# From unit 4 on, two units share one SSD stretch on TensorE; the recurrent half of Y in 32x64 tiles, the first MLP matmul in 512 columns, PSUM banks chosen step by step, and a new order from unit 3

## The chip, the cores and the metric

One core of a Trainium2 chip runs one program. The figure of merit is device time per execution in microseconds (us), a median of several runs. The engines are TensorE (PE in the profile; its weight loads are PEld), VectorE (DVE), ScalarE (ACT), GpSimd (POOL) and SyncE (SP), which issues nearly all DMAs. Each engine works through its own instructions in the order in which they were written, and waits where a semaphore tells it to. TensorE writes only to PSUM, here eight banks of 128 partitions by 512 fp32 columns.

## The reference

Two stages follow each other. The first is a chunked state-space scan (SSD) over x of shape (4 batches, 8 heads, 768 steps, 32 features) with state size 16:

```python
L = np.exp(cum[:, :, :, None] - cum[:, :, None, :]) * causal
M = np.einsum('bhin,bhjn->bhij', Cc, Bc) * L
y_intra = np.einsum('bhij,bhjd->bhid', M, xc)
y_inter = np.einsum('bhin,bhnd->bhid', Cc, state) * np.exp(cum)[..., None]
y = y_intra + y_inter
state = decay_full * state + sum_j B_j x_j decay_from_j
```

Its output, regrouped to 3072 tokens by 256 columns, goes through an MLP: `h = x @ w_in` (256 to 2048), `g = gelu_tanh(h)`, `out = g @ w_out` (2048 to 256), fp32 in HBM, bf16 on TensorE.

## The kernel before, in words

The kernel uses chunks of 128 steps: 24 chunks in 4 batches, two chunks to a unit, so 12 units of T = 256 tokens. Unit u holds chunks 2u and 2u+1; a batch is three units. The decays are folded into B and C beforehand (`mul`), so that the SSD part of a unit is plain matmuls:

- **G.u** (`f_G`): C times B per head pair, weights of 32 rows by 128 columns, 256 columns streamed, eight matmuls into the PSUM pair ga, gb. **M.u.0** and **M.u.1** on VectorE mask ga and gb into bf16.
- **D.u** (`f_D`): the chunk's contribution to the state, four matmuls per chunk (none for a batch's last chunk). **S.u.k** (`f_S`, VectorE) adds it to the running state; **SP.c** (`f_SP`, VectorE) spreads the state of chunk c over the heads in bf16.
- **Y.u** (`f_Y`): per chunk eight matmuls of the masked scores with x (intra) and, unless the chunk is a batch's first, eight of the spread state with C (inter), all with weights of 128 rows by 32 columns and 128 streamed columns, accumulated in the bank yb. **yev.u** evicts the bank to xm, the MLP's input.
- **s1.u.i** (`f_s1`, i = 0 to 7): the first MLP matmul, four matmuls of 256 columns into one bank of pool hp (two buffers). **gelu.u.i** on ScalarE evicts that bank to gT.
- **s2.u.k.q** (`f_s2`): a quarter of the second MLP matmul of chunk 2u+k, four matmuls of 256 columns into a bank o_ps (in the last four chunks partly yb). **oev.c** evicts chunk c's result, **store.c** writes it to HBM.
- For batches 2 and 3, B and C are prepared through DRAM: **load_bc.b** reads them, **mul** scales them, **load_wr** writes the scaled copy to DRAM, **load_tr** reads it back transposed (ch, bh), **load_bn** reads it back untransposed (bn, which D needs), and **F.b** on VectorE splits ch into ce, which G needs.

Every one of these pieces is a named step. The string ORDERED lists all steps in the order in which their instructions are written, with the engine where there is a choice (`:A`, `:D`, `:P`). Nothing else sets the order within an engine. The framework adds the semaphore waits that the tiles' reads and writes call for. From unit 3 on, before, Y.u, D.u+1 and G.u+1 are welded into one step, so that each unit has one SSD stretch on TensorE between steps of the MLP.

In the code before, `f_G` is around L618, `f_D` L651, `f_Y` L673 and L682, `f_S` L697 and L699, `f_SP` L706, `f_s1` L732, `f_gelu` L736, `f_s2` L750, `f_store` L760, and L337, L339 and L341 are the copies on ScalarE, GpSimd and VectorE.

Of the kernel before, what the change touches and what calls it, by code (L numbers as in the profile page):

```python
# [1001 lines left out]
```

## Time and profile before

| | |
|---|---|
| time, median of 3 runs | 117.47 us (116.52 to 118.22) |
| span of the profiled execution, first to last instruction | 115.0 us |
| TensorE busy | 108.1 us, 94% of the span |
| VectorE, ScalarE, GpSimd busy | 68.0, 70.0, 25.9 us |
| granted TensorE clock | 1.000 throughout |

The profile gives one execution. Its span leaves out what lies ahead of the first and behind the last instruction; the three timed runs lie 1.5 to 3.2 us above that span, and the profiled execution has no time of its own beside it. "Busy" of TensorE counts from a matmul's issue to the modelled end of its result, which is later than the moment at which the next matmul may start: the distance between the starts of consecutive matmuls is the pace, and the duration is the pace plus the way through the array.

### The profile page before, as it was taken

Reading aid. Unit: us, or ns where it says so; the run is one execution under the profiler, and the core shown is the slowest. Engines: PE = TensorE matmul, PEld = TensorE weight load, DVE = VectorE, ACT = ScalarE, POOL = GpSimd, SP = SyncE. Lnnn points to the kernel's source line nnn. Section 1 sums busy time; section 2 is a strip of 40 time slices with the busy share of each in tenths; the row PEclk is TensorE's granted clock in tenths of the full one; section 3 lists DMA queues with packets and bytes.
Section 4 is the critical chain, followed back from the end, with each engine's and each line's share of the span. In section 5 each row is a group of like instructions: output and inputs, shape, how many; then the busy total and the mean of one; then the engine's idle time right before and its main releaser. Section 6 shows DMA issues by size and latency. Waiting matters only on the chain.

```text
span 115.0 us, 3377 instructions
## 1 busy us (share of the span) xinstructions
PE 108.1 (94%) x1421; PEld 91.7 (80%) x1421; DVE 68.0 (59%) x136; ACT 70.0 (61%) x133; POOL 25.9 (23%) x54
## 2 busy tenths in 40 slices
PE   6979888999999999999999999999999999999990
PEld 2235566888879997989989899889898898999970
DVE  6889998989974755969448491186750851010100
ACT  3159687687654455747675876456495576758620
POOL 7636856806439020201120030000000000000000
PEclk9999999999999999999999999999999999999999
DMA  0999979979994779997556922350003020001113
GB/s 24 231 309 336 332 212 191 317 132 321 215 238 101 141 177 203 196 272 175 88 131 150 209 62 85 111 86 0 0 9 134 0 71 26 0 0 55 42 62 120
DMA packets 43103, 16.00 MB, mean 139 GB/s; under 512 B 36688, under 2 KB 41552, under 8 KB 43088
## 3 DMA queue, kind: packets, MB, share of 16 engines
q1 hardware_dynamic: 42896, 15.70, 55.3%
q8 instruction: 11, 0.18, 0.7%
q10 hardware_dynamic: 192, 0.09, 0.3%
q14 instruction: 4, 0.03, 0.1%
HBM read 11.07 MB, written 3.93 MB: 130 GB/s over the span
## 4 chain that ended last, share of the span: by engine, by line
PE 82%; DVE 5%; DMA 4%; SPq 3%; issue 2%; ACT 2%; DVEq 0%
PE hp L732 35%; PE o_ps L750 34%; DMA x_t<-in_x_dram 4%; PE yb L750 3%; PE yb L673 3%; PE ga L618 2%; PE yb L682 2%; DVE m L628 1%; DVE sp_new L706 1%; SPq L164 1%; ACT gT L736 1%; SPq L151 1%; SPq L160 1%; DVE rt L364 1%; DVE r_t L354 1%
## 5 line engine op out<-in xcount | busy, mean ns | idle before, releaser
L736 ACT ACTIVATE gT<-hp 128x512 bf16<-128x512 f32 x96 | 54.3, 596 | 28.9 <-PE hp L732 28.6
L732 PE MATMUL hp<-xm,w_in_sb 128*128 128x256 bf16 x384 | 53.4, 273 | 1.1 <-DVE s_new L699 0.5
L750 PE MATMUL o_ps<-w_out_sb,gT 128*128 128x256 bf16 x352 | 46.8, 273 | 0.0
L732 PEld LDWEIGHTS <-w_in_sb 128*128 128x128 bf16 x384 | 41.2, 114 | 4.0 <-issue 2.7
L750 PEld LDWEIGHTS <-gT 128*128 128x128 bf16 x384 | 37.4, 98 | 4.1 <-issue 0.4
L341 DVE COPY o_sb<-o_ps 128x256 f32<-128x256 f32 x12 | 5.1, 425 | 26.9 <-PE o_ps L750 26.9
L628 DVE TENSOR_TENSOR m<-ga,tri 128x1024 bf16<-128x1024 f32 x12 | 14.6, 1216 | 0.0
L628 DVE TENSOR_TENSOR m<-gb,tri 128x1024 bf16<-128x1024 f32 x11 | 13.4, 1216 | 0.0
L339 POOL CAST x<-x_t 128x512 bf16<-128x512 f32 x8 | 6.0, 756 | 28.1 <-DMA x_t<-in_x_dram 24.4
L706 DVE SCALAR_TENSOR_TENSOR sp_new<-s_new,pend,bmask 128x256 bf16<-128x256 f32 x17 | 8.0, 483 | 0.1
L699 DVE SCALAR_TENSOR_TENSOR s_new<-s_new,pend,hp 128x64 f32<-128x64 f32 x13 | 3.5, 272 | 7.4 <-PE hp L651 7.3
L720 PE MATMUL yb<-wz 128*128 128x512 bf16 (+2 forms) x21 | 6.6, 455 | 1.1 <-DVE warm L226 1.1
L337 ACT ACTIVATE o_sb<-o_ps 128x256 f32<-128x256 f32 x10 | 3.8, 383 | 5.1 <-PE o_ps L750 3.8
L682 PE MATMUL yb<-m,x 128*32 128x128 bf16 x192 | 6.1, 220 | 0.0
L337 ACT ACTIVATE xm<-yb 128x512 bf16<-128x512 f32 x8 | 4.8, 596 | 1.3 <-PE hp L651 0.7
L720 PEld LDWEIGHTS <-wz 128*128 128x128 bf16 x21 | 2.3, 116 | 4.1 <-issue 2.1
L673 PE MATMUL yb<-ce,sp_new 128*32 128x128 bf16 x160 | 5.3, 221 | 0.0
L339 POOL CAST w_out_sb<-wf 128x512 bf16<-128x512 f32 x6 | 4.1, 692 | 4.7 <-DMA wf<-in_moe_w_out_dram 4.7
L618 PE MATMUL ga<-ce,bh 32*128 32x256 bf16 x48 | 4.7, 273 | 0.3 <-DVE par L289 0.3
L618 PE MATMUL gb<-ce,bh 32*128 32x256 bf16 x48 | 4.7, 273 | 0.0
L750 PE MATMUL yb<-w_out_sb,gT 128*128 128x256 bf16 x32 | 4.5, 273 | 0.0
L682 PEld LDWEIGHTS <-x 128*32 128x32 bf16 x192 | 3.7, 96 | 0.9 <-issue 0.9
(114 smaller groups left out, 75.0 us busy)
## 6 DMA issues: line engine op xcount, KB each, us to landing
out_dram<-o_sb SPq DMA_DIRECT2D x24, 128.0 KB, 2.0
x_t<-in_x_dram SPq DMA_DIRECT2D x20, 128.0 KB, 3.9
wf<-in_moe_w_in_dram SPq DMA_DIRECT2D x4, 512.0 KB, 7.0
wf<-in_moe_w_out_dram SPq DMA_DIRECT2D x4, 512.0 KB, 7.1
bc_t<-in_C_dram SPq DMA_DIRECT2D x3, 384.0 KB, 4.7
bc_t<-in_B_dram SPq DMA_DIRECT2D x3, 384.0 KB, 5.7
scr<-bc SPq DMA_DIRECT2D x4, 192.0 KB, 2.3
x_t<-in_x_dram SPq DMA_DIRECT2D x1, 512.0 KB, 4.4
```

What stands on the lines that cost most here:

```text
L337: nc.scalar.activation(o, i, AF.Copy)
L339: nc.gpsimd.tensor_copy(out=o, in_=i)
L341: nc.vector.tensor_copy(out=o, in_=i)
L618: nc.tensor.matmul(out=gbank(g)[:, 256 * k:256 * k + 256], lhsT=bh_of(2 * u + k)[gs], rhs=ce_of(2 * u + k)[gs], start=True, stop=True, til ...
L628: nc.vector.tensor_tensor(out=m_of(u)[:, 2 * i:2 * i + 2].rearrange("p g k e t -> p (g k e) t"), in0=gx[i].rearrange("p g (k t) -> p (g k) ...
L673: nc.tensor.matmul(out=y4[32 * j:32 * j + 32, k, w], lhsT=sp[:, 32 * h:32 * h + 32], rhs=ce_of(gc)[:, h % 2], start=first(j), stop=False, ...
L682: nc.tensor.matmul(out=y4[32 * j:32 * j + 32, k, w], lhsT=X16[u][:, k, 32 * h:32 * h + 32], rhs=m[:, h // 2, h % 2, :], start=first(j), st ...
L706: nc.vector.scalar_tensor_tensor(out=sp_new.rearrange("p (g d) -> p g d", g=4), in0=(XN[0][:, H * D:H * D + 64] if gc == 0 else state[("s" ...
L720: nc.tensor.matmul(out=t[:, 0:m * 128], lhsT=wz, rhs=w3.to_broadcast([128, m, 128]), start=True, stop=True, skip_group_check=True)
L732: nc.tensor.matmul(out=hp[:, j * T:(j + 1) * T], lhsT=w_in_k[:, w, q, k], rhs=xm[:, w, u * T:(u + 1) * T], start=(w == 0), stop=(w == 1))
L736: nc.scalar.activation(gts[u][:, 2 * i:2 * i + 2], hps.pop((u, i)).rearrange("p (j t) -> p j t", j=2), AF.Gelu_apprx_tanh)
L750: nc.tensor.matmul(out=ops[gc], lhsT=gts[u][:, fi, k * Q:(k + 1) * Q], rhs=w_out_sb[:, fi, :], start=(fi == 0 and (u > 0 or k == 0)), stop ...
```

## The change

From unit 4 on (`U2 = 4`) units are taken in pairs (4,5), (6,7), (8,9), (10,11):

- Y of a pair becomes **Yi.u** (all intra matmuls, as before 128 rows by 32 columns) for both units and then **YI.u** (all inter matmuls, now weights of 32 rows by 64 columns, four a chunk instead of eight). A pair's Y fills two whole banks, one per half w of the columns, each evicted by one **yew.u.w**, w = 0 on ScalarE and w = 1 on VectorE.
- D of an odd unit from 7 on is written into the bank of the even unit's D, at columns 128 to 255. D of both units stands between Yi and YI of the pair ahead.
- G from unit 6 on is sixteen matmuls of 32 rows by 64 columns instead of eight of 32 by 128. G of the even unit stands behind YI; G of the odd unit stands alone further on, as do G.5 and D.5.
- s1 of a pair is 16 steps of two matmuls of 512 columns, over both units' tokens, instead of 2 times 8 steps of four matmuls of 256. gelu is as large as before.
- The three pools hp (2 banks), o_ps (1) and yb (1) become four fixed banks a, b, o and y; ORDERED names the bank behind an @ where it isn't the usual one.
- ORDERED names the same steps in the same order up to s1.2.6, the step behind oev.0; from there the order is new.

```diff
+    U2 = 4
+    PT = 2 * T
-    GT_BUFS = 5
+    GT_BUFS = 2
-    pso = ctx.enter_context(tc.tile_pool(name="pso", bufs=1, space=bass.MemoryType.PSUM))
-    psh = ctx.enter_context(tc.tile_pool(name="psh", bufs=2, space=bass.MemoryType.PSUM))
...
-    yb = ps1.tile([128, 512], FP32, name="yb")
+    bank = {k: ps1.tile([128, 512], FP32, name=f"bank_{k}") for k in "aboy"}
+    yb = bank["y"]
+    def take(pool):
+        if at:
+            return bank[at.pop(0)]
+        if pool == "hp":
+            hp_turn.append(0)
+            return bank["ba"[len(hp_turn) % 2]]
+        return bank[pool]
...
     def f_G(u):
+        if u > U2 + 1:
+            for k in range(2):
+                for i, g in [(i, g) for i in range(2) for g in range(4)]:
+                    gs, js = slice(32 * g, 32 * g + 32), slice(64 * i, 64 * i + 64)
+                    nc.tensor.matmul(out=gbank(g)[js, 256 * k:256 * k + 256], lhsT=bh_of(2 * u + k)[gs, js],
+                                     rhs=ce_of(2 * u + k)[gs], start=True, stop=True,
+                                     tile_position=(32 * g, 64 * i), skip_group_check=True)
+            return
...
     def f_D(u):
-        DT[u] = psh.tile([128, 512], FP32, name="hp")
+        if u < U2 + 2 or u % 2 == 0:
+            DT["bank"] = take("hp")
+        DT[u] = DT["bank"][:, 0:128] if u < U2 + 2 or u % 2 == 0 else DT["bank"][:, 128:256]
...
+    def f_Yi(u):
+        v = u % 2
+        YT[u] = (take("y"), take("o")) if v == 0 else YT[u - 1]
+        for w, k, j in [(w, k, j) for w in range(2) for k in range(2) for j in range(4)]:
+            h, t = 4 * w + j, v * T + k * Q
+            nc.tensor.matmul(out=YT[u][w][32 * j:32 * j + 32, t:t + Q],
+                             lhsT=X16[u][:, k, 32 * h:32 * h + 32], rhs=MT[u][:, h // 2, k, h % 2],
+                             start=(v == 0 and k == 0), stop=True, tile_position=(0, 32 * j), skip_group_check=True)
+
+    def f_YI(u):
+        for k in range(2):
+            gc = 2 * u + k
+            if gc % CPB == 0:
+                continue
+            sp = state.pop(("sp", gc - 1))
+            t = u % 2 * T + k * Q
+            for g in range(4):
+                gs, i = slice(32 * g, 32 * g + 32), g % 2
+                nc.tensor.matmul(out=YT[u][g // 2][64 * i:64 * i + 64, t:t + Q],
+                                 lhsT=sp[gs, 64 * g:64 * g + 64], rhs=ch_of(gc)[gs], start=False, stop=True,
+                                 tile_position=(32 * g, 64 * i), skip_group_check=True)
+
+    def f_yew(u, w, eng):
+        copy(eng, xm[:, w, u * T:u * T + PT], YT[u][w])
...
+    def f_s1(u, i):
+        gt(u)
+        hp = hps[(u, i)] = take("hp")
+        if u < U2:
...
+        else:
+            q, k = divmod(i, 4)
             for w in range(2):
+                nc.tensor.matmul(out=hp, lhsT=w_in_k[:, w, q, k], rhs=xm[:, w, u * T:u * T + PT],
+                                 start=(w == 0), stop=(w == 1))
...
-    for u in range(3, NU - 1):
-        y = steps[f"Y.{u}"]
-        gone = [steps.pop(f"D.{u + 1}"), steps.pop(f"G.{u + 1}")]
...
-gelu.11.5 store.16 s1.11.7 s2.10.1.3 store.20 oev.21:D gelu.11.6 s2.11.0.1.yb gelu.11.7
+M.5.1 load_bc.3.1 load_bc.3.0 s1.3.6 s1.3.7 s2.2.1.1 store.4 gelu.3.6 gelu.3.7 Yi.4@ya Yi.5 F.2 D.6@b
+SP.10 S.6.0 D.7 mul.3.1:P YI.4 S.6.1 YI.5 G.6 s2.2.1.2 s2.2.1.3 yew.4.1 S.7.0 yew.4.0 s1.4.0@a S.7.1
...
+s2.11.0.2 s2.11.0.3 oev.22:A s2.10.0.3 oev.21:A oev.23:A store.17 oev.20:A store.20 store.23 store.22
+store.21
```

What stands in the engines' queues at three places follows. A row gives the line, the operation, the tile written and read (with the number of its buffer) and what the instruction waits for, an engine or a DMA queue by name; rows that only repeat are left out.

**The SSD stretch on TensorE and the state on VectorE.** First TensorE before, from the end of Y.5 through D.6 (hp_1166) to G.6:

```order
L673 MATMUL yb_148<-ce_712,sp_new_1084 32x128
L682 MATMUL yb_148<-m_1079,x16_967 32x128
L651 LDWEIGHTS bn_1103 [waits Activation_49,DMAHW6_49]
L651 MATMUL hp_1166<-x16_1096,bn_1103 32x64 [waits Pool_49]
L618 LDWEIGHTS bh_1106 [waits DMAHW7_49]
L618 MATMUL ga_146<-ce_1126,bh_1106 128x256 [waits DVE_49]
L618 MATMUL gb_147<-ce_1126,bh_1106 128x256
```

The same place after the change, from the end of Yi.5 through D.6 (x16_930), D.7 (x16_874), YI.4 and YI.5 to G.6:

```order
L717 MATMUL bank_a_142<-m_932,x16_867 32x128
L675 LDWEIGHTS bn_955 [waits Activation_49,DMAHW3_49]
L675 MATMUL bank_b_143<-x16_930,bn_955 32x64 [waits Pool_49]
L675 MATMUL bank_b_143<-x16_874,bn_955 32x64 [waits DVE_49]
L730 MATMUL bank_y_145<-ch_671,sp_new_783 64x128
L730 MATMUL bank_a_142<-ch_671,sp_new_783 64x128
L633 LDWEIGHTS bh_953 [waits DMAHW2_49]
L633 MATMUL ga_140<-ce_1020,bh_953 64x256
```

VectorE after the change at that place: F.2 (twice), SP.10, S.6.0, S.6.1, yew.4.1 and S.7.0.

```order
L548 TENSOR_SCALAR ce_1020<-ch_941,par_116 128x768 [waits DMAHW1_49]
L755 TENSOR_SCALAR sp_new_1031<-s_new_951,pend_128,bmask_110 128x256 [waits DVE_49]
L746 COPY s_new_1033<-bank_b_143 128x64 [waits PE_49,Activation_49]
L748 TENSOR_SCALAR s_new_1053<-s_new_1033,pend_128,bank_b_143 128x64 [waits DVE_49,PE_49]
L351 COPY xm_139<-bank_a_142 128x512 [waits PE_49]
L748 TENSOR_SCALAR s_new_1088<-s_new_1053,pend_128,bank_b_143 128x64 [waits DVE_49]
```

D.7 now follows D.6 in the same bank, with S.6.0 written between the two, and its first matmul carries a wait on VectorE; S.6.1, written behind D.7, waits for TensorE once more. The pairs (6,7) and (8,9) have the same form with D.8, S.8.0, D.9 and D.10, S.10.0, D.11; in the last pair nothing of the kind is left.

**SP's queue ahead of batch 2's transposes.** Before:

```order
L177 DMA x_t_957<-in_x_dram 128x8x32 [waits DMAHW0_49]
L513 DMA scr21_1046<-bc16_949 128x768 [waits DMAHW1_49,Pool_49]
L177 DMA x_t_1061<-in_x_dram 128x8x32 [waits DMAHW2_49]
L177 DMA x_t_1061<-in_x_dram 128x8x32 [waits DMAHW3_49]
L513 DMA scr20_1064<-bc16_949 128x768 [waits DMAHW4_49,Pool_49]
L520 DMA_TRANSPOSE ch_1081<-scr21_1046 128x768 [waits DMAHW5_49,DMAHW1_49]
L525 DMA bn_1103<-scr20_1064 128x6x128 [waits DMAHW6_49,DMAHW4_49]
```

After:

```order
L175 DMA x_t_775<-in_x_dram 128x8x32 [waits DMAHW1_49]
L175 DMA x_t_778<-in_x_dram 128x8x32 [waits DMAHW3_49]
L822 DMA out_0_dram<-o_sb_763 128x256 [waits DMAHW5_49,DVE_49]
L523 DMA scr21_865<-bc16_808 128x768 [waits DMAHW6_49,DVE_49]
L523 DMA scr20_876<-bc16_808 128x768 [waits DMAHW7_49,Pool_49]
L822 DMA out_0_dram<-o_sb_781 128x256 [waits DMAHW0_49,Activation_49]
L530 DMA_TRANSPOSE ch_941<-scr21_865 128x768 [waits DMAHW6_49,DMAHW1_49]
L530 DMA_TRANSPOSE bh_953<-scr20_876 128x768 [waits DMAHW7_49,DMAHW2_49]
L535 DMA bn_955<-scr20_876 128x6x128 [waits DMAHW3_49]
```

The loads of x for units 6 and 7 (two DMAs each) and two stores now stand ahead of the transposes, and bn is read behind both transposes instead of between them.

**The end, on ScalarE and SP.** Before, ScalarE's last two evictions (chunks 22 and 23), and SP's last stores (22, 21, 18, 23):

```order
L337 ACTIVATE o_sb_2239<-yb_148 128x256 [waits DMAHW1_49,PE_49,Activation_49]
L337 ACTIVATE o_sb_2241<-o_ps_2221 128x256 [waits DMAHW2_49,PE_49]
L760 DMA out_0_dram<-o_sb_2239 128x256 [waits DMAHW5_49,Activation_49]
L760 DMA out_0_dram<-o_sb_2205 128x256 [waits DMAHW6_49,DVE_49]
L760 DMA out_0_dram<-o_sb_2037 128x256 [waits DMAHW7_49]
L760 DMA out_0_dram<-o_sb_2241 128x256 [waits DMAHW0_49,Activation_49]
```

After, chunks 22, 21, 23 and 20 on ScalarE, and the stores in the order 20, 23, 22, 21:

```order
L347 ACTIVATE o_sb_1949<-bank_a_142 128x256 [waits DMAHW7_49,DMAHW2_49,PE_49]
L347 ACTIVATE o_sb_1955<-bank_y_145 128x256 [waits DMAHW0_49,Activation_49]
L347 ACTIVATE o_sb_1957<-bank_b_143 128x256 [waits DMAHW5_49,DMAHW1_49,DVE_49]
L347 ACTIVATE o_sb_1960<-bank_o_144 128x256 [waits DMAHW2_49,PE_49]
L822 DMA out_0_dram<-o_sb_1960 128x256 [waits DMAHW5_49,Activation_49]
L822 DMA out_0_dram<-o_sb_1957 128x256 [waits DMAHW6_49]
L822 DMA out_0_dram<-o_sb_1949 128x256 [waits DMAHW7_49]
L822 DMA out_0_dram<-o_sb_1955 128x256 [waits DMAHW0_49]
```

The last four chunks are now evicted by ScalarE one after the other, and the first of the last four stores is that of the chunk that is evicted last. TensorE's last step is s2.10.0.3 (chunk 20), and the step ahead of it s2.11.0.3 (chunk 22).

256 lines of the change are left out of this document (137 added, 119 removed).

## The prediction

> **What bounds the kernel now.** I read the page first.
>
> ```profile
> PE 108.1 (94%) x1421; PEld 91.7 (80%) x1421; DVE 68.0 (59%) x136; ACT 70.0 (61%) x133; POOL 25.9 (23%) x54
> PE 82%; DVE 5%; DMA 4%; SPq 3%; issue 2%; ACT 2%; DVEq 0%
> ```
>
> TensorE is busy 94% of the span and is 82% of the chain that ended last. The waits tell the same: nobody keeps TensorE waiting after the start. So the span behaves as TensorE's queue plus a short tail, and an edit is worth what it takes from that queue or puts into it. TensorE's timeline gives the prices (start, duration; a pace is the distance between starts).
>
> ```profile
> 32.23 0.60 PE L732 MATMUL hp<-xm,w_in_sb 128*128 128x256 bf16 x4
> 43.65 0.60 PE L750 MATMUL o_ps<-w_out_sb,gT 128*128 128x256 bf16 x4
> 44.18 0.29 PE L673 MATMUL yb<-ce,sp_new 128*32 128x128 bf16 x8
> 44.30 0.28 PE L682 MATMUL yb<-m,x 128*32 128x128 bf16 x8
> 44.41 0.28 PE L673 MATMUL yb<-ce,sp_new 128*32 128x128 bf16 x8
> 44.52 0.28 PE L682 MATMUL yb<-m,x 128*32 128x128 bf16 x8
> 44.63 0.20 PE L651 MATMUL hp<-x,bn 128*32 128x64 bf16 x4
> 44.77 0.28 PE L618 MATMUL ga<-ce,bh 32*128 32x256 bf16 x2
> 44.89 0.27 PE L618 MATMUL ga<-ce,bh 32*128 32x256 bf16 x2
> 45.10 0.63 PE L732 MATMUL hp<-xm,w_in_sb 128*128 128x256 bf16 x4
> 110.01 1.91 PE L750 MATMUL o_ps<-w_out_sb,gT 128*128 128x256 bf16 x16
> ```
>
> The last row: sixteen matmuls take 1.91 us with one way through the array (0.27), so 256 columns cost 1.64 / 15 = 0.1092 us, a step of four 0.437. In the SSD stretch eight matmuls of Y cost 0.1125, since four run side by side; D with four costs 0.03, with eight about 0.055; G costs 0.23 (0.12 from one chunk to the next and 0.11). Each change of tile shape costs a gap: 0.09 going in (43.65 + 0.437 = 44.09, Y starts at 44.18), 0.11 from D to G, 0.10 going out.
>
> **The change, part by part.** Up to s1.2.6 both kernels issue the same; it starts at 32.23, so the new part starts at 32.67 on both. Before, TensorE then works to 110.01 + 16 x 0.1092 = 111.76, which is 79.1 us. It holds 73 s1 steps and 88 s2 steps, 161 x 0.437 = 70.3, and so 8.8 us for nine SSD stretches (Y.3 to Y.11), stalls included.
>
> *Stretches after the change.* G.4, D.4 and Y.3 stay together: 0.09 + 0.23 + 0.11 + 0.055 + 3 x 0.1125 + 0.10 = 0.93. G.5, G.7, G.9 and G.11 stand alone, each 0.09 + 0.23 + 0.10 = 0.42, together 1.68; D.5 alone is 0.22. A pair's stretch is 0.09 in, 0.45 for Yi (32 matmuls, as Y), 0.055 to 0.11 for two D's, 0.11 to the new shape, YI, G 0.23, 0.10 out. No row shows 32x64 tiles. The nearest are G's 32x128, four at once, and these 32x32 tiles:
>
> ```profile
> 9.68 0.20 PE L596 MATMUL o_ps<-x4b,bc0s 32*32 32x64 bf16 x1
> 9.80 0.19 PE L596 MATMUL hp<-x4b,bc0s 32*32 32x64 bf16 x1
> ```
>
> Thirty-two matmuls of 64 columns, over two row groups and four column groups, start within 0.12 us: eight at once. I take eight at once for the new G (0.23, as before) and four for YI (0.055 a chunk, 0.22 for four). With one at least serial pair each, G would cost 0.46 and YI 0.44; with six G's and 14 chunks of YI that is 6 x 0.23 + 14 x 0.055 = 2.1 more, the upper bound; below nothing it can't go, since eight tiles are all that a 32x64 array has and a chunk's YI has only four matmuls. The four pairs then cost 1.31, 1.22, 1.22 and 0.98 (the last has no D and no G). All stretches: 0.93 + 1.68 + 0.22 + 4.73 = 7.6, a gain of **1.2 us**. [...]
>
> *s1 in 512 columns.* The nearest row is the filler behind 32x32 tiles, four matmuls of 512 and one of 128 columns:
>
> ```profile
> 9.92 1.09 PE L720 MATMUL yb<-wz 128*128 128x512 bf16 x5
> L720 PE MATMUL yb<-wz 128*128 128x128 bf16 x1 | 0.2, 219 | 0.0
> ```
>
> (1.09 - 0.219) / 4 = 0.218 per 512 columns against 2 x 0.1092: over 128 matmuls **0.1 us** gained, with the rounding of the row between nothing and 0.4 (the last filler may be 10 ns off).
>
> *The wait between two D's.* D.7, D.9 and D.11 write the bank that S.6.0, S.8.0 and S.10.0 read, and the first matmul of D.7 waits for VectorE; S.6.1, behind D.7, waits for TensorE again although D.6 wrote all that it needs. So the bank is guarded as a whole, and TensorE stands still for D.6's way out, S.6.0 and the way back. The rows:
>
> ```profile
> 57.97 0.23 PE L651 MATMUL hp<-x,bn 128*32 128x64 bf16 x8
> 58.29 0.60 DVE L699 SCALAR_TENSOR_TENSOR s_new<-s_new,pend,hp 128x64 f32<-128x64 f32 x2 [0.58 <-PE hp L651]
> L699 DVE SCALAR_TENSOR_TENSOR s_new<-s_new,pend,hp 128x64 f32<-128x64 f32 x13 | 3.5, 272 | 7.4 <-PE hp L651 7.3
> 13.33 0.28 DVE L699 SCALAR_TENSOR_TENSOR s_new<-s_new,pendq,hp 128x64 f32<-128x64 f32 x1
> 13.66 1.03 PE L732 MATMUL hp<-xm,w_in_sb 128*128 128x256 bf16 x8 [0.31 <-DVE s_new L699]
> ```
>
> 0.32 from D's start to S's, 0.27 for S, 0.05 from S's end (13.61) to TensorE (13.66): 0.64, of which D itself fills 0.055. Three times 0.58 is **1.7 us** lost. Queued behind are YI, G, the MLP steps and, through them, ScalarE: nothing hides it. Its lower bound is 0, if the wait names something long past; upper 2.5, if VectorE is late.
>
> *The b and n loads of batch 2.* D.6 needs bn.2. In the stream it is due 32.67 + 0.93 + 0.42 + 0.22 + 23 x 0.437 + 0.54 (Yi) = 44.8. SP before:
>
> ```profile
> 30.34 3.82 SPq L177 DMA_DIRECT2D x_t<-in_x_dram  x2
> 36.13 0.36 SPq L513 DMA_DIRECT2D scr<-bc  x1
> 36.54 2.11 SPq L177 DMA_DIRECT2D x_t<-in_x_dram  x2
> 38.75 0.56 SPq L513 DMA_DIRECT2D scr<-bc  x1
> 39.61 1.23 SPq L520 DMA_TRANSPOSE ch<-scr  x1
> 41.23 0.38 SPq L525 DMA_DIRECT2D bn<-scr  x1
> 44.04 1.15 SPq L177 DMA_DIRECT2D x_t<-in_x_dram  x2
> 48.62 2.61 SPq L177 DMA_DIRECT2D x_t<-in_x_dram  x2
> 42.99 1.00 SPq L760 DMA_DIRECT2D out_dram<-o_sb  x2
> DMA to landing us min/median/max: 2.8/3.0/3.2
> ```
>
> The last row is that of bn. After the change SP is free at 34.16, issues two pairs of x loads (1.15 to 2.61 a pair, say 1.5), a store (0.5) and the first scratch write at 37.7. As 36.13 to 39.61 shows with other issues between, a write lands in some 2.3 us: the transposes start at 40.0, take 1.23 each, bn.2 is issued at 42.5 and lands at 45.5. D.6 waits **0.7 us**, between 0 and 2.9 (x loads at 2.61 a pair).
>
> *Bank a or b reused after three steps.* s1 on b, s2, s1 on a, s1 on b again leaves 0.436 + 0.437 + 0.436 = 1.31 from one use to the next.
>
> ```profile
> 104.34 0.60 PE L732 MATMUL hp<-xm,w_in_sb 128*128 128x256 bf16 x4
> 104.97 0.60 ACT L736 ACTIVATE gT<-hp 128x512 bf16<-128x512 f32 x1
> ```
>
> gelu starts 0.63 after its s1, takes 0.60, and TensorE restarts in about 0.05: 1.28. That holds as long as ScalarE has nothing else in hand; an eviction (0.38) ahead of a gelu shows in full. I count 0, with 0.8 as the upper end.
>
> *The tail.*
>
> ```profile
> 111.96 0.38 ACT L337 ACTIVATE o_sb<-o_ps 128x256 f32<-128x256 f32 x1 [1.31 <-PE o_ps L750]
> L760 SPq DMA_DIRECT2D out_dram<-o_sb x24: 332/403/1264, 43.0 to 112.4; - x24
> ```
>
> Before, one eviction (0.38) follows the modelled end of TensorE, 110.01 + 1.91 = E, and the last store is issued at 112.4, E + 0.5; the span ends 2.6 later. After, chunk 22 is complete at E - 0.44, and ScalarE evicts 22, 21, 23 and 20 in a row, 4 x 0.38 from E - 0.40: done at E + 1.1. Only then is store.20 issued, and behind it 23, 22 and 21 at 0.5 each (42.99 above: two in 1.00). The last is issued at E + 2.6 instead of E + 0.5, or at E + 1.9 if evictions overlap by 0.1 and each issue takes the row's least, 0.33. I take **2.0 us** longer, bounds 1.4 and 2.4. What hid the other evictions and stores before was TensorE's work; behind E nothing does.
>
> **Sum:** -1.2 - 0.1 + 1.7 + 0.7 + 0 + 2.0 = +3.1 on the profiled 115.0: a span of 118.1. The median of the runs shown is 2.5 above that span; adding the same, 117.47 + 3.1 = **120.6 us**, 2.6% slower. A measurement of this kernel tells about 2% from no change, 115.1 to 119.8.
>
> **Rivals.**
>
> 1. *Not slower: the wait in D.7, D.9 and D.11 is over when it is reached.* The point that decides is whether S.6.0 is the instruction waited for. Then 1.7 falls away: 118.9, within 2%. For it: S.6.0 reads other columns than D.7 writes. Against it: S.6.1's second wait.
> 2. *32x64 tiles run fewer at once:* +2.1, 122.7. For it: no row of this shape; against: 32x32 tiles ran eight at once.
> 3. *Batch 2 is late by DMA:* D.6 waits 2.9 instead of 0.7: 122.8. For it: an x pair took 3.82 at 30.34; against: the queue was empty from 34.16 to 36.13.
> 4. *The tail is shorter,* evictions overlapping and issues at their least, 1.4 instead of 2.0: 120.0. Against it: pairs of stores took 0.5 each.
> 5. *The weight loads set the pace of s1, not the columns.* A load takes 114 ns, about the pace of 109:
>
> ```profile
> L732 PEld LDWEIGHTS <-w_in_sb 128*128 128x128 bf16 x384 | 41.2, 114 | 4.0 <-issue 2.7
> ```
>
> If so, 512 columns follow each other at 0.114 too, 128 x (0.218 - 0.114) = 13 us go, and the time is about 107. Against it: the filler, which loads weights for each matmul too, at 0.218. [...]
>
> **How the numbers follow.** Forecast 0.43, rival 1 0.17, rival 2 0.10, rival 3 0.18, rival 4 0.09, rival 5 0.03. The range runs from 117.8 (rival 1, with the tail and s1 at their better ends and the DMA in time) to 123.0 (rivals 2 and 3). Below 115.1 lies rival 5 and the coming together of all better ends, 0.05. Within 2% lie nearly all of rival 1 (0.16), the lower third of the forecast (0.13) and a third of rival 4 (0.03), 0.32. Slower is the rest, 0.63.
>
> **What would show it.** TensorE's timeline after the change: 0.218 between the starts of s1's matmuls; 16 G matmuls within 0.23; a gap of about 0.6 between D.6 and D.7, D.8 and D.9, D.10 and D.11, put down to VectorE's s_new; a wait of D.6 on a DMA; TensorE's end at 111.92 + 1.1, and 5.1 us from there to the span's end instead of 3.1. A gap-free stretch or stores that overlap would make me wrong.

## The result and the profile after

The changed kernel takes **122.62 us** (median of 4 runs, 122.03 to 124.39), the kernel before, measured beside it, 117.84 us (116.52 to 118.70). The ratio is **1.044, 95% interval 1.035 to 1.053**. The forecast was 120.6 us, 2.0 us too low. The profiled execution took 122.17 us with a span of 120.4 us, 5.4 us more than the 115.0 of before. Of the eight executions of this kernel measured here and in experiment 1, three took 122.0 to 122.2 us at a mean granted clock of 0.991 to 1.000 and five took 123.1 to 125.4 us at 0.967 to 0.982; the ratios leave out every execution that took over 1.5% longer than the fastest of its kernel.

The page after, its busy line and its chain of waits:

```profile
PE 108.5 (90%) x1285; PEld 77.5 (64%) x1285; DVE 69.4 (58%) x135; ACT 70.3 (58%) x135; POOL 24.8 (21%) x53
PE 61%; DVE 15%; DMA 9%; SPq 4%; issue 4%; ACT 3%; ACTq 0%; DVEq 0%
```

TensorE was 82% of that chain and is now 61%; VectorE went from 5 to 15% and DMA from 4 to 9%. So TensorE now waits. Its timeline after names the places; these are the rows of D.6, D.7, D.9 and D.11 with their idle time in brackets:

```profile
47.51 0.24 PE L675 MATMUL bank_b<-x,bn 128*32 128x64 bf16 x8 [0.41 <-DMA bn<-scr]
48.16 0.24 PE L675 MATMUL bank_b<-x,bn 128*32 128x64 bf16 x8 [0.40 <-DVE s_new L746]
62.83 0.24 PE L675 MATMUL bank_b<-x,bn 128*32 128x64 bf16 x8 [0.54 <-DVE s_new L748]
79.12 0.21 PE L675 MATMUL bank_b<-x,bn 128*32 128x64 bf16 x4 [0.45 <-DVE s_new L748]
```

The bracket counts from the modelled end of the matmul ahead. From start to start D.7 comes 0.65 us after D.6, D.9 0.75 after D.8 (62.08), D.11 0.68 after D.10 (78.44). Without a wait a D of eight matmuls takes some 0.06: in experiment 2 sixteen of them take 0.30 us, eight 0.24. The tail, from the timeline of TensorE, ScalarE and SP:

```profile
114.85 0.60 PE L812 MATMUL bank_o<-w_out_sb,gT 128*128 128x256 bf16 x4
115.05 0.38 ACT L347 ACTIVATE o_sb<-bank_a 128x256 f32<-128x256 f32 x1 [3.77 <-PE bank_a L812]
...
115.86 0.40 ACT L347 ACTIVATE o_sb<-bank_o 128x256 f32<-128x256 f32 x1
116.28 1.80 SPq L822 DMA_DIRECT2D out_dram<-o_sb  x4
```

TensorE's modelled end is 114.85 + 0.60 = 115.45. Four evictions follow at 0.27 from start to start, then four stores. The span ends at 120.4, 4.95 behind TensorE; before it was 3.08 (115.0 less 111.92).

One loss stands where the two programs are equal: s1.2.6 starts at 33.81 instead of 32.23. VectorE and GpSimd show why; the last row is the group of all sp_new, which averaged 483 ns before:

```profile
33.81 0.60 PE L786 MATMUL bank_a<-xm,w_in_sb 128*128 128x256 bf16 x4
21.41 1.48 DVE L755 SCALAR_TENSOR_TENSOR sp_new<-s_new,pend,bmask 128x256 bf16<-128x256 f32 x1 [0.17 <-DVE s_new L748]
21.11 1.50 POOL L509 TENSOR_TENSOR bc<-bc_t,pt 128x768 bf16<-128x768 f32 x1 [0.68 <-DMA bc_t<-in_C_dram]
L755 DVE SCALAR_TENSOR_TENSOR sp_new<-s_new,pend,bmask 128x256 bf16<-128x256 f32 x17 | 10.2, 603 | 0.2 <-DVE s_new L748 0.2
```

SP.4 took 1.48 us instead of 0.48, beside GpSimd's mul.1.1, which had started 0.3 us earlier. In the profile of before the order was the other way round, SP.4 at 20.93 and GpSimd at 21.46.

### The profile page after: what moved, and what is told of

The parts are those of the page before. It is cut to its first block, busy times and chain, and to the rows that moved or that the text cites. A ratio compares the mean times of both kernels' runs of the same rounds, so it can differ in the third digit from the quotient of the medians.

```text
span 120.4 us, 3123 instructions
## 1 busy us (share of the span) xinstructions
PE 108.5 (90%) x1285; PEld 77.5 (64%) x1285; DVE 69.4 (58%) x135; ACT 70.3 (58%) x135; POOL 24.8 (21%) x53
## 4 chain that ended last, share of the span: by engine, by line
PE 61%; DVE 15%; DMA 9%; SPq 4%; issue 4%; ACT 3%; ACTq 0%; DVEq 0%
PE bank_o L812 14%; PE bank_y L812 12%; PE bank_b L791 11%; PE bank_a L791 10%; DVE m L650 4%; DMA x_t<-in_x_dram 4%; DVE sp_new L755 3%; DMA bn<-scr 3%; DMA scr<-bc 2%; SPq L530 2%; PE bank_o L791 2%; DVE bc L509 2%; PE bank_a L786 2%; PE bank_b L786 2%; DVE s_new L748 2%
## 5 line engine op out<-in xcount | busy, mean ns | idle before, releaser
L812 PE MATMUL bank_o<-w_out_sb,gT 128*128 128x256 bf16 x192 | 26.7, 273 | 0.0
L800 ACT ACTIVATE gT<-bank_a 128x512 bf16<-128x512 f32 x27 | 16.1, 597 | 12.6 <-PE bank_a L791 12.5
L812 PE MATMUL bank_y<-w_out_sb,gT 128*128 128x256 bf16 x160 | 22.0, 273 | 0.0
L800 ACT ACTIVATE gT<-bank_b 128x512 bf16<-128x512 f32 x29 | 17.3, 595 | 4.4 <-PE bank_b L791 4.3
L791 PEld LDWEIGHTS <-w_in_sb 128*128 128x128 bf16 x128 | 14.1, 114 | 6.1 <-issue 0.6
L791 PE MATMUL bank_b<-xm,w_in_sb 128*128 128x512 bf16 x58 | 17.3, 379 | 0.0
L791 PE MATMUL bank_a<-xm,w_in_sb 128*128 128x512 bf16 x54 | 16.1, 379 | 0.0
L786 PEld LDWEIGHTS <-w_in_sb 128*128 128x128 bf16 x128 | 13.4, 114 | 2.8 <-issue 1.5
L797 ACT ACTIVATE gT<-bank_a 128x512 bf16<-128x512 f32 x16 | 9.5, 595 | 6.0 <-PE bank_a L786 5.8
L797 ACT ACTIVATE gT<-bank_b 128x512 bf16<-128x512 f32 x16 | 9.5, 595 | 2.2 <-PE bank_b L786 2.1
L786 PE MATMUL bank_a<-xm,w_in_sb 128*128 128x256 bf16 x64 | 9.6, 272 | 1.0 <-ACT gT L797 0.4
L786 PE MATMUL bank_b<-xm,w_in_sb 128*128 128x256 bf16 x64 | 9.7, 274 | 0.2 <-DVE s_new L748 0.2
L769 PE MATMUL bank_y<-wz 128*128 128x512 bf16 (+2 forms) x21 | 7.0, 473 | 1.1 <-DVE warm L224 1.1
```

What stands on the lines that cost most here:

```text
L769: nc.tensor.matmul(out=t[:, 0:m * 128], lhsT=wz, rhs=w3.to_broadcast([128, m, 128]), start=True, stop=True, skip_group_check=True)
L786: nc.tensor.matmul(out=hp[:, j * T:(j + 1) * T], lhsT=w_in_k[:, w, q, k], rhs=xm[:, w, u * T:(u + 1) * T], start=(w == 0), stop=(w == 1))
L791: nc.tensor.matmul(out=hp, lhsT=w_in_k[:, w, q, k], rhs=xm[:, w, u * T:u * T + PT], start=(w == 0), stop=(w == 1))
L797: nc.scalar.activation(gts[u][:, 2 * i:2 * i + 2], hp.rearrange("p (j t) -> p j t", j=2), AF.Gelu_apprx_tanh)
L800: nc.scalar.activation(gts[("p", u)][:, i], hp, AF.Gelu_apprx_tanh)
L812: nc.tensor.matmul(out=ops[gc], lhsT=gts[u][:, fi, k * Q:(k + 1) * Q], rhs=w_out_sb[:, fi, :], start=(fi == 0 and (u > 0 or k == 0)), stop ...
```

## The experiments

The edits are in ORDERED unless said otherwise; only the pieces that change are shown, and a wide gap in a line stands for steps left out. "After" and "before" are the two kernels of this document.

**1. After and before once more.** No edit; this tells what belongs to the change and what to one execution.

> The kernel after the change once more, unaltered, to see whether the 1.58 us that its unchanged head lost (s1.2.6 starts at 33.81 instead of 32.23) come back. Theory 1, the timing of one execution: which of VectorE and GpSimd gets to its instruction first varies, so s1.2.6 starts somewhere between 32.2 and 33.9, and in some profiles of this head near 32.2. Theory 2, the changed program does it every time: 33.6 to 34.0 in every profile with this head. Time 122.6 by both, 121 if theory 1 holds and this execution is a lucky one.

> The kernel before once more, unaltered, for a second look at its head. Theory 1 (timing of one execution): s1.2.6 starts anywhere between 32.2 and 33.9, and where it is late an sp_new of VectorE lasts 1 us or more beside a tensor instruction of GpSimd. Theory 2 (systematic): 32.1 to 32.4 again.

The second execution of after, TensorE's rows of s1.2.6, s1.2.7, D.6 and D.11; then s1.2.6 in the second execution of before:

```profile
32.45 0.60 PE L786 MATMUL bank_a<-xm,w_in_sb 128*128 128x256 bf16 x4
34.04 0.60 PE L786 MATMUL bank_a<-xm,w_in_sb 128*128 128x256 bf16 x4
47.38 0.24 PE L675 MATMUL bank_b<-x,bn 128*32 128x64 bf16 x8 [1.88 <-DMA bn<-scr]
79.00 0.21 PE L675 MATMUL bank_b<-x,bn 128*32 128x64 bf16 x4 [0.45 <-DVE s_new L748]
```

```profile
32.04 0.60 PE L732 MATMUL hp<-xm,w_in_sb 128*128 128x256 bf16 x4
```

Theory 1 holds: here SP.4 took 0.48 us and the head was in time. And yet the span was 120.3 us, 0.1 less than with the late head, because D.6 waited 1.88 us for bn instead of 0.41. D.6 started at 47.4 both times. So the time lost in the head came back in a shorter wait at D.6; batch 2's way through DRAM sets when D.6 can start. That it started at the same moment both times is in part chance: the first scratch write came at 38.89 behind mul.2.1, which the late head had pushed back, and at 39.59 behind SP's queue (the rows are in the part on the prediction). The sum over both executions, in us against the profile of before:

| part | forecast | first | second |
|---|---|---|---|
| start of s1.2.6 | 0 | +1.58 | +0.22 |
| D.6 later than due | +0.7 | +0.58 | +2.05 |
| D.7, D.9, D.11 | +1.7 | +1.94 | +1.94 |
| stretches and s1 | -1.3 | -0.57 | -0.81 |
| tail | +2.0 | +1.87 | +1.90 |
| span | +3.1 | +5.4 | +5.3 |

(D.6 is due 0.55 behind the end of the step ahead, 46.38 and 44.78. The fourth row is what is left of TensorE's end, +3.53 and +3.40, after the rows above it.)

**2. Both D's ahead of S.**

```diff
-D.6@b SP.10 S.6.0 D.7        D.8@b S.8.0 D.9     D.10@b S.10.0 D.11
+D.6@b SP.10 D.7 S.6.0        D.8@b D.9 S.8.0     D.10@b D.11 S.10.0
```

> After, with S.6.0, S.8.0 and S.10.0 written behind D.7, D.9 and D.11 instead of ahead of them; nothing else moves. Theory A (the bank is guarded as a whole, so that D of the odd unit stands still for S of the even one): the gaps of 0.65, 0.75 and 0.68 us between the D's of a pair go to under 0.05 each, the span falls by 1.9 us less what VectorE, now behind by one S, gives back: YI waits for nobody there, so all of 1.9; time 120.7, against 122.6. Rival (rival 1 of the prediction, or a wait that another one takes over at the same place, such as the spread state that YI needs): the gaps move to YI and the time stays at 122.6.

TensorE's rows at the three places:

```profile
47.64 0.30 PE L675 MATMUL bank_b<-x,bn 128*32 128x64 bf16 x16 [2.25 <-DMA bn<-scr]
62.39 0.24 PE L675 MATMUL bank_b<-x,bn 128*32 128x64 bf16 x8 [0.55 <-POOL x L349]
78.01 0.26 PE L675 MATMUL bank_b<-x,bn 128*32 128x64 bf16 x12
```

At the first and third place the two D's run through as one group: the wait was S.6.0 and S.10.0, and it was a matter of order alone. At the second a new wait takes the place of the old one in full, D.9 again 0.75 after D.8 (61.64): it needs unit 9's x, whose cast on GpSimd had waited for its load until 61.73. From D.6 to the last step it is 66.14 us (47.64 to 113.78) against 67.34 in the second execution of after (47.38 to 114.72): 1.2 gained of 1.9. The ratio to before is 1.037 (1.028 to 1.047).

**3. The tail spread.**

```diff
-... s2.10.1.3 s2.11.1.0@b s2.11.1.1 s2.11.1.2 s2.11.1.3 s2.11.0.2 s2.11.0.3 oev.22:A s2.10.0.3
-oev.21:A oev.23:A store.17 oev.20:A store.20 store.23 store.22 store.21
+... s2.10.1.3 store.17 oev.21:D store.21 s2.11.1.0@b s2.11.1.1 s2.11.1.2 s2.11.1.3
+oev.23:D store.23 s2.11.0.2 s2.11.0.3 oev.22:D store.22 s2.10.0.3 oev.20:A store.20
```

> After, with the last four evictions spread: chunk 21 (VectorE) and its store behind s2.10.1.3, chunk 23 (VectorE) and its store behind s2.11.1.3, chunk 22 on VectorE and chunk 20 on ScalarE as each is complete, each store behind its own eviction. Theory T (nothing hides evictions and stores behind TensorE's end): from the end of TensorE to the end of the span 3.1 to 3.4 us instead of 4.95, time 120.9 to 121.1 against 122.6. Rival: the last store's landing is held up by something that doesn't depend on the order (the store's own DMA), then 4.5 or more, and 122.2.

TensorE's last step and the only eviction behind it, then D.6; in the second fence three windows of 1 us from there on (length, busy time of PE, PEld, DVE, ACT and POOL with their instructions, the granted clock, DMA share, GB/s):

```profile
117.00 0.60 PE L811 MATMUL bank_o<-w_out_sb,gT 128*128 128x256 bf16 x4
117.64 0.38 ACT L346 ACTIVATE o_sb<-bank_o 128x256 f32<-128x256 f32 x1 [4.21 <-PE bank_o L811]
...
48.34 0.24 PE L674 MATMUL bank_b<-x,bn 128*32 128x64 bf16 x8 [3.00 <-DMA bn<-scr]
```

```profile
48.00:49.00 1.00, 0.26 (x12) 0.16 (x13) 0.23 (x1) 0.00 (x0) 0.00 (x0) 0.79 1.15 307
50.00:51.00 1.00, 1.00 (x12) 0.58 (x5) 0.96 (x3) 0.48 (x1) 1.00 (x1) 0.50 0.20 50
52.00:53.00 1.00, 0.95 (x6) 0.55 (x6) 1.00 (x2) 0.39 (x1) 0.00 (x0) 1.00 0.70 255
```

Theory T holds: from TensorE's end (117.60) to the end of the span (120.8) it is 3.2 us instead of 4.95. But TensorE itself ended later. D.6 waited 3.00 us, since bn, issued at 44.16, took 4.1 us to land where it took 3.0 in both profiles of after; nothing in the edit explains that. Right behind the wait the granted clock was 0.50 until about 52; from D.7 (48.98) to D.9 (64.98) it took 16.00 us, against 14.67 in the second execution of after (48.03 to 62.70). So two losses follow each other here: the wait, and 1.3 us of slower matmuls behind it. Behind the 1.88 us of waiting in the second execution of after the clock stayed at 1.00. The time was 1.039 of before (1.027 to 1.050).

**4. bn read between the transposes.**

```diff
-load_tr.2.0 load_bn.2
+load_bn.2 load_tr.2.0
```

> After, with bn of batch 2 read back between the two transposes instead of behind both, as the kernel before does; nothing else moves. Theory D (batch 2's chain of DMAs sets when D.6 can start: 47.4 to 48.3 us in every profile so far, whatever the head did): SP issues bn 1.33 us earlier, it lands 1.3 us earlier, D.6 starts at 46.0 to 47.0, and the span falls by 0.9 to 1.3 us: time 121.0 to 121.6 where after has 122.3. Rival H (the slower head is what costs, D.6's wait only its echo): D.6 starts no earlier than 47.2 and the time stays within 0.4 us of 122.3. A second rival: bh, now read last, makes G.6 wait instead, and the time stays.

A miss in time: the ratio was 1.043 (1.036 to 1.051), that of after, and not the 0.9 to 1.3 us less that theory D asked for. The one profile can't tell why: the execution had a mean granted clock of 0.959, s1.2.6 started at 38.98 already, and the stream came so late that D.6 (51.86) waited for nobody. What this edit does alone stays open.

**5. x of units 6 and 7 behind the scratch writes.**

```diff
-load_bc.2.0 load_x.5 load_x.6 load_x.7        gelu.3.0 castx.7.None:P load_wr.2.0
+load_bc.2.0 load_x.5                          gelu.3.0 load_wr.2.0 load_x.6 load_x.7
-castx.6.None:P
+castx.6.None:P castx.7.None:P
```

> After, with the loads of x for units 6 and 7 (and the cast of unit 7) moved behind batch 2's two scratch writes; bn stays behind both transposes. Theory D: SP no longer spends 5 us on these loads ahead of the writes, and B of batch 2 shares the DMA engines with two x loads instead of six; the first write is issued at 36.4 to 37.5 instead of 38.9 to 40.0, bn lands at 44.8 to 45.8, D.6 waits 0 to 0.4 us, and the span falls by 1.5 to 2.0 us: time 120.3 to 120.9. The granted clock, 0.79 in 48 to 56 us of the spread-tail run where D.6 had waited 3.0 us, stays at 1.00 there. Rival 1: the multiplications of B and C on VectorE and GpSimd set the writes, not SP's queue; then the writes stay at 38.5 or later and the time at 122. Rival 2: x of units 6 and 7 comes too late, and D.6 or D.7 waits for a cast of x instead.

mul.2.1 on VectorE, then SP's scratch writes and the read of bn, then D.6:

```profile
37.07 1.59 DVE L508 TENSOR_TENSOR bc<-bc_t,pt 128x768 bf16<-128x768 f32 x1
38.69 1.33 SPq L522 DMA_DIRECT2D scr<-bc  x2
46.46 0.57 SPq L534 DMA_DIRECT2D bn<-scr  x1
49.58 0.24 PE L674 MATMUL bank_b<-x,bn 128*32 128x64 bf16 x8 [2.34 <-DMA bn<-scr]
```

A miss: 1.064 (1.058 to 1.070), slower than after. Rival 1 was right in this profile. The first write follows mul.2.1's end (38.66; the head was late in this profile, s1.2.6 at 34.19), not SP's queue, and the four x loads, 3.07 us of issue, now stand between the writes and the transposes, so that bn is issued some 2 us later than in after.

**6. The chain of batch 2 at four places.**

```diff
-oev.1 SP.7 store.0 G.4        load_x.5 load_x.6 load_x.7       load_tr.2.0 load_bn.2
+oev.1 G.4                     load_x.5 load_x.6                load_bn.2 load_tr.2.0
-M.4.1 s2.1.0.0@o s2.1.0.1 mul.2.1:D M.4.0                      load_wr.2.0
+mul.2.1:D M.4.1 s2.1.0.0@o s2.1.0.1 M.4.0 SP.7                 load_wr.2.0 load_x.7 store.0
```

> After, with batch 2's chain shortened at four places: mul.2.1 on VectorE ahead of M.4.1 instead of behind it, SP.7 behind M.4.0, x of unit 7 and store.0 behind the two scratch writes instead of ahead, and bn between the transposes. Moving x of units 6 and 7 alone had not worked: the writes stayed at 38.7, because mul.2.1 ended only at 38.6 on VectorE, and the four x loads then stood ahead of the transposes. Theory D: first write at 36.0 to 37.5, bn issued by 42.5, landed by 45.5, D.6 waits 0 to 0.5 us; against the 0.4 to 3.0 of after this is 1.0 to 2.0 us: a span of 118.3 to 119.5 and a time of 120.0 to 121.2. And since a wait of some 3 us at D.6 is what had brought the clock to 0.5, the granted clock stays above 0.99 in all runs. Rival: DMA traffic, not the order, sets the landing of B (35.7) and of bn, and D.6 still starts at 47 or later: 122.

SP's first scratch writes and read of bn; TensorE at D.7 and at D.9:

```profile
35.72 1.69 SPq L522 DMA_DIRECT2D scr<-bc  x2
42.33 0.52 SPq L534 DMA_DIRECT2D bn<-scr  x1
46.01 0.24 PE L674 MATMUL bank_b<-x,bn 128*32 128x64 bf16 x8 [0.41 <-DVE s_new L745]
61.13 0.24 PE L674 MATMUL bank_b<-x,bn 128*32 128x64 bf16 x8 [0.80 <-POOL x L348]
```

Theory D holds. (The cast of unit 7's x moves too, behind that of unit 6; the edits were not tried one by one.) The write is 3 to 4 us earlier, D.6 starts at 45.36, as it is due, and D.7, 0.65 behind it, at 46.01 instead of 48.0 to 49.0. The span was 118.7, the time 120.53 us, 1.033 of before (1.027 to 1.038), and the granted clock stayed between 0.988 and 1.000 in all four runs. D.9 again waits for unit 9's x, 0.8 us.

**7. The head mended, and nothing else.** One edit in after, and the same edit in before:

```diff
-SP.4 load_bc.1.0 M.2.1 M.2.0
+load_bc.1.0 M.2.1 M.2.0 SP.4
```

> After, with SP.4 on VectorE behind M.2.1 and M.2.0 instead of ahead of them, so that beside GpSimd's long multiplication of C (mul.1.1, 1.5 us at 21.1 to 21.8) VectorE works on M, which reads PSUM, and not on an sp_new that reads only SBUF. In the profiles so far SP.4 took 0.48 us where it started before that multiplication (s1.2.6 then at 32.0 to 32.5) and 1.1 to 1.6 where it started after it (s1.2.6 at 33.6 to 34.2). Theory (each holds the other up, and the first to start wins): SP.4 takes 0.4 to 0.5 us whichever comes first, s1.2.6 starts at 32.0 to 33.0. What it gives to the span: by theory D (batch 2's DMA chain sets D.6) nothing, since D.6's wait grows by what the head gains, span 120 to 121.5, time 122 to 123; by rival H (the head is what costs) 1.4 us in the profiles with a late head, a median of 121.3.

> Before, with the one edit of the head: SP.4 on VectorE behind M.2.1 and M.2.0. Theory (the head's 1.5 us come and go with which of VectorE and GpSimd starts first, in both kernels): nothing in the executions where VectorE came first, 1.4 us in the others; the runs of before spread from 116.5 to 119, these from 116.4 to 117.5, the median 0.3 to 0.9 us lower. Rival (only the changed program has the late head): no difference.

In after: TensorE's s1.2.6 and D.6, and three of the windows behind D.6.

```profile
32.27 0.60 PE L786 MATMUL bank_a<-xm,w_in_sb 128*128 128x256 bf16 x4
47.92 0.24 PE L675 MATMUL bank_b<-x,bn 128*32 128x64 bf16 x8 [2.61 <-DMA bn<-scr]
```

```profile
49.00:50.00 1.00, 1.00 (x35) 0.73 (x16) 0.91 (x3) 0.60 (x1) 0.49 (x1) 1.00 1.02 253
50.00:51.00 1.00, 1.00 (x6) 0.53 (x4) 0.66 (x3) 0.38 (x1) 1.00 (x1) 0.52 0.06 18
52.00:53.00 1.00, 1.00 (x6) 0.72 (x5) 1.00 (x2) 0.68 (x2) 0.00 (x0) 0.50 0.94 335
```

The head was in time, and nothing was gained: 125.0 us, 1.060 (1.052 to 1.067), where theory D had asked for 122 to 123. That the edit itself makes after slower is not shown. The second execution of after had its head in time without the edit and a span of 120.3 us, 2.2 less than the 122.5 here. The two profiles differ in two places: bn, issued at 44.19, took 3.7 us to land instead of 3.0, so that D.6 started 0.54 us later; and behind that wait of 2.61 us the clock fell to 0.50, so that D.7 to D.9 (48.57 to 64.91) took 16.34 us instead of 14.67. All four executions had a mean granted clock of 0.970 to 0.983, as five of the eight of after had. In before the edit changes nothing: 0.999 (0.996 to 1.002), with 116.77 us against 116.87. In both profiles of before VectorE was first, so the edit had nothing to mend. Why GpSimd was first in some profiles of kernels with after's head is open.

**8. s1 in 256 columns.** In `f_s1`, four matmuls of 256 columns for each pair step.

> After, with s1 of the pairs back in 256 columns (four matmuls a step), all else as after. Theory: a step takes 4 x 0.1092 = 0.437 instead of 0.433 us; over 64 steps 0.24 us, TensorE's last matmul 0.2 to 0.3 us later from D.6 on; no other effect. Rival: weight loads share in the pace, so that twice as many loads cost 1 us or more; or the 512 columns are what brings the lower clock.

D.11 and the last step, first of this kernel; of after's second execution D.11 is above, and its last step starts at 114.72:

```profile
80.30 0.21 PE L675 MATMUL bank_b<-x,bn 128*32 128x64 bf16 x4 [0.45 <-DVE s_new L748]
...
116.18 0.60 PE L812 MATMUL bank_o<-w_out_sb,gT 128*128 128x256 bf16 x4
```

From D.11 to there it is 35.88 us against 35.72: 0.16 over 32 steps, 5 ns a step, some 0.3 us over 64. The theory holds in size, and the weight loads don't set the pace. The time of this one run, 123.5 us, holds waits at D.6 (2.60) and D.9 (1.02) that have nothing to do with the columns.

**9. G in 32x128 tiles in all units,** on the kernel of 6 (in `f_G`, the sixteen-matmul branch is never taken).

> After with the shortened chain of batch 2, and G in 32x128 tiles in all units, as before: eight matmuls instead of sixteen. Theory (sixteen 32x64 tiles run eight at once, so that G takes as long as before): the lone G's take 0.42 to 0.46 us from the step ahead to the step behind in both forms, and the pairs' stretches differ by less than 0.1; rival 2 of the prediction (fewer at once): the lone G's are shorter by 0.2 us than with 32x64, some 1.2 us in all.

The lone G.7's first row and the step behind it, with 32x64 tiles (kernel of 6):

```profile
53.12 0.29 PE L632 MATMUL ga<-ce,bh 32*64 32x256 bf16 x2
53.48 0.62 PE L790 MATMUL bank_y<-xm,w_in_sb 128*128 128x512 bf16 x2
```

With 32x128 tiles G.7 started at 54.03 and the next step at 54.37: 0.34 us against 0.36 here. Sixteen matmuls in the new tiles take 0.02 us longer than eight in the old ones, far from the 0.2 of rival 2.

**10. The edits together.** First 2, 3, 4 and 5 with unit 9's x beside unit 8's; then 2, 3, 6, 7 with that x; then also batch 3:

```diff
-load_wr.3.1 mul.3.0:D     load_tr.3.1 load_tr.3.0 ... load_bn.3     castx.8.None:D F.3     S.9.1 G.8
+load_wr.3.1 mul.3.0:P     load_bn.3 load_tr.3.1 load_tr.3.0         castx.8.None:D         S.9.1 G.8 F.3
```

> After, with all four edits at once: S behind both D's, the tail spread, x of units 6 and 7 behind the scratch writes, bn between the transposes; and x of unit 9 loaded beside unit 8's, since D.9 waited 0.55 us for it once S was out of the way. If the losses are separate they add: 1.9 for the D's, 1.7 for the tail, 1.9 for batch 2, together 5.5 us, a span of 114.8 and a time of 116.6, level with the kernel before (117.5, its lowest 116.5); what the stretches save is then all that is left of the change. If they overlap (a wait taken away shows the next one), 118 to 120.

> After, with the shortened chain of batch 2, S behind both D's, the spread tail, x of unit 9 beside unit 8's, and SP.4 behind M.2.0. If the losses add up: D's 1.9, tail 1.7, batch 2 1.0 to 2.0 us off 120.3: a span of 114.7 to 115.5, a time of 116.4 to 117.2, against 117.2 to 117.5 for before (0.99 to 1.00 of it); with no waits left on TensorE what remains is the unchanged stream less 0.6 for stretches and s1. If one loss hides behind another: 118 or more.

> The combined kernel once more, with batch 3's chain shortened like batch 2's: mul.3.0 on GpSimd instead of VectorE, where it had waited 3.4 us for B's DMA and held up M.6 and, behind it, G.7 on TensorE by 1.44 us; bn of batch 3 ahead of its transposes; F.3 on VectorE behind G.8. Theory (waits add up): G.7 waits no more, the span of the profile falls from 117.2 to 115.0 to 116.0, the median from 118.5 to 116.6 to 117.5, level with before (116.9), since the stretches and s1 give 0.5 and the head and the tail cost what they do before. Rival (the next wait on a DMA shows): D.9 waits for bn or x of batch 3 by 1 us or more, and the time stays above 118.

The first gave 1.020 (1.014 to 1.027): experiment 5's detour was in it, and D.6 waited 1.23 us. The second gave 1.010 (1.006 to 1.014), 118.48 us. Its profile has a new wait, at G.7, and on VectorE the instruction that brought it, mul.3.0:

```profile
54.86 0.29 PE L631 MATMUL ga<-ce,bh 32*64 32x256 bf16 x2 [1.44 <-DVE m L648]
...
51.58 0.96 DVE L507 TENSOR_TENSOR bc<-bc_t,rt 128x768 bf16<-128x768 f32 x1 [3.36 <-DMA bc_t<-in_B_dram]
```

VectorE waited 3.36 us for B of batch 3, M.6 stood behind that, and G.7 needs M.6 to have read its banks. The third takes this away: **116.98 us against 116.69, ratio 1.0005 (0.997 to 1.004)**. The one wait left on TensorE from s1.2.6 on, and its last step:

```profile
45.69 0.30 PE L673 MATMUL bank_b<-x,bn 128*32 128x64 bf16 x16 [0.30 <-DMA bn<-scr]
...
111.39 0.60 PE L810 MATMUL bank_o<-w_out_sb,gT 128*128 128x256 bf16 x4
```

So the whole loss of the change lies in the order in which its steps are written and the engine that a few of them are given; with these mended, the pairs, the new tiles and the 512 columns are level with before, no better. Whether yet another order would make them better is open.

## Why the prediction was wrong, step by step

The sign was right and the size was not: 2.6% forecast, 4.4% measured, inside the range of 117.8 to 123.0. In spans the miss is larger than the time shows: +3.1 us forecast on 115.0, +5.4 and +5.3 measured. The forecast added 2.5 us from the span to the time, and every execution of the record that has both shows 1.7 to 1.9; by luck this took back 0.7 us of the miss.

- **The failed step is "issues two pairs of x loads (1.15 to 2.61 a pair, say 1.5), a store (0.5) and the first scratch write at 37.7" and the D.6 wait of 0.7 us that follows from it.** The mechanism was right, SP's time ahead of the write was mis-sized. By the forecast the six loads and store.0 take 3.8 + 3.0 + 0.5 = 7.3 us of SP's queue. In the five profiles with this order whose head was in time (the second of after, experiments 2, 3, 7 and 8) they took 9.3 to 9.8: loads of 7.0 to 7.1 us and a store of 2.3 to 2.8, or loads of 8.5 to 8.7 and a store of 0.6. The write followed 0.1 later, at 39.5 to 40.0, when mul.2.1 had long ended (36.1 to 36.3). What held SP that long is not shown. The forecast also left out that the write waits for mul.2.1 on VectorE; where the head was late, as in the first profile of after, that is what set it (37.92 + 0.95 = 38.87). In both cases bn was issued at 44.2 to 45.0 instead of 42.5, and D.6 started at 47.4 to 48.3 instead of 45.5. Experiment 6, which takes a pair of loads and the store from ahead of the write, had the write at 35.72 and no wait at D.6. SP and mul.2.1 of after, first profile, then second:

```profile
29.66 7.16 SPq L175 DMA_DIRECT2D x_t<-in_x_dram  x6
36.93 1.10 SPq L822 DMA_DIRECT2D out_dram<-o_sb  x1
37.92 0.95 DVE L509 TENSOR_TENSOR bc<-bc_t,pt 128x768 bf16<-128x768 f32 x1
38.89 1.59 SPq L523 DMA_DIRECT2D scr<-bc  x2
...
44.45 0.57 SPq L535 DMA_DIRECT2D bn<-scr  x1
```

```profile
30.23 8.52 SPq L175 DMA_DIRECT2D x_t<-in_x_dram  x6
35.33 0.95 DVE L509 TENSOR_TENSOR bc<-bc_t,pt 128x768 bf16<-128x768 f32 x1
38.87 0.62 SPq L822 DMA_DIRECT2D out_dram<-o_sb  x1
39.59 0.38 SPq L523 DMA_DIRECT2D scr<-bc  x1
...
44.30 0.57 SPq L535 DMA_DIRECT2D bn<-scr  x1
```

- **Rival 3 (chance 0.18)** has the mechanism, a batch 2 that is late by DMA. Its size was too large, 2.9 us at D.6 against 2.05 with the head in time. Its span, 115.0 + 5.3 = 120.3, is the measured one by luck: what it has too much at D.6 was lost in the stretches (0.5), the D's and the head (0.2 each). What it did not have is the price of the lower clock, 1.3 us in the profile of experiment 3.
- **The write's landing, 2.3 us:** the rows quoted for it (36.13 to 39.61) are 3.5 us apart, with an x pair between. The value itself is near what was measured, 2.0 to 3.0 from the write to the first transpose.
- **"Up to s1.2.6 both kernels issue the same; it starts at 32.23."** Equal instructions, but not equal times: 32.3 to 32.6 in most profiles of this head, 33.8 to 34.2 in three, 38.98 in that of experiment 4. In after the late head only moved the wait from D.6 to the head and left the span as it was.
- **Stretches, -1.2:** mis-sized. With s1's 0.3 taken out of the table's fourth row, 0.3 to 0.5 remain. A pair's stretch without waits was as forecast (1.25 for 1.22 in the second and third pair of the last combined kernel, 1.00 for 0.98 in the fourth; 1.35 for 1.31 in the first pair of after). The 8.8 us of before were too high, since only 8.6 lie between its MLP steps and the rest is rounding of 161 steps. Unit 3's stretch took 1.15 (34.04 - 32.45 - 0.44) instead of 0.93: s1.2.7 uses s1.2.6's bank again, and gelu.2.6 stood on ScalarE behind the eviction of chunk 1. That is the case that "bank a or b reused", counted at 0, had named with its price.
- **s1, -0.1:** right in kind, -0.3 measured.
- **The wait between two D's, +1.7:** near, 1.94, and by the mechanism told, as experiment 2 shows; rival 1 is refuted. At the second place another wait as long stood behind it, for unit 9's x, which the prediction did not see.
- **The tail, +2.0:** near, 1.87; evictions follow each other at 0.27, not 0.38, and the stores take 0.45 each.
- **Rivals 2 and 5** are refuted by G's 0.36 against 0.34 (experiment 9) and s1's 5 ns a step (experiment 8). YI stands in the pairs' stretches, which took what was forecast with four of its matmuls at once.

## What to carry to other kernels

A load that is cast, scaled, written, transposed and read back has to be followed from its first issue to the instruction that needs it; here, what stood ahead of one of its links, on SP or on VectorE, was paid for at the far end (D.6 waited 1.88 us in the second execution of after and for nobody in experiment 6), and time won ahead of that point was only waited away there (0.41 us of wait behind the late head, 1.88 behind the early one). A bank that two matmuls share coupled them here to the reader written between them: 0.65 us from D.6 to D.7, and one group of 0.30 once the reader stood behind both. And the last evictions and stores want to be written where TensorE still has work to hide them: 4.95 us from TensorE's end to the end of the span became 3.2.

## What was not expected of the hardware

- Behind a wait of 3.0 us on TensorE (experiment 3) the granted clock was 0.50 to about 52, and D.7 to D.9 took 16.00 us instead of 14.67; behind waits of 1.88, 2.25 and 2.34 us (the second execution of after, experiments 2 and 5) it stayed at 1.00. Behind 2.61 us it fell to 0.50 (experiment 7), behind 2.60 us it stayed at 1.00 (experiment 8). What decides is not shown.
- The same read of 192 KB, bn of batch 2, took 3.0 to 3.1 us from its issue to the start of the D.6 that waited for it in seven profiles (after twice, experiments 2, 5 and 8, the second and third kernel of 10), 3.6 in one (the first kernel of 10), and 3.7 and 4.2 in the two (experiments 7 and 3) in which the clock fell behind the wait for it. What held it up is open.
- VectorE's sp_new, which reads only SBUF, took 1.48 us instead of 0.48 when GpSimd's multiplication of 1.50 us had started 0.3 us ahead of it (first profile of after: GpSimd's instruction ends at 22.61, VectorE's at 22.89). VectorE's M, which reads PSUM, took its 1.22 us beside the same multiplication in the profile of before (21.33, GpSimd at 21.46). What in the two cases makes the difference is not shown.
